# An induced-set attention with a gated convolution on one Trainium2 core: groups of 508 tokens with their own halo, h summed on VectorE, f16 output products in the last batch

## The chip, the core and the metric

The kernel runs on one core of a Trainium2 chip. TensorE (PE) multiplies matrices into PSUM, VectorE (DVE), ScalarE (ACT) and GpSimd (POOL) work elementwise, and SyncE's queue (SP) and ACT's queue issue the DMAs. The metric is the time on the device in microseconds (us), the median of several runs. A profiled execution gives the trace that the text reads.

## What is computed

```python
# x: (4, 12800, 128), inducing I: (32, 128); everything float32, weights come as float64
def mab(q, kv):
    s = scale * (q @ kv.T);  s = s - s.max(-1)
    a = exp(s);  a /= a.sum(-1) + 1e-09
    return a @ kv
h = mab(I, x)                  # per batch: 32 rows from 12800 tokens
y = mab(x, h)                  # 12800 tokens, softmax over 32
gate = sigmoid(causal 5-tap depthwise convolution of y by conv_w)
out  = (gate * (y @ w_val)) @ w_out
```

## The kernel before

The host passes x twice, in two layouts: `xT`, channels by tokens, and `xk`, tokens by channels. Each batch is cut into seven units: six big ones of 4 x 512 tokens and a small one of 4 x 128 (first in batch 0, last in the others; in stage 1 of batch 0 it is read last). Four groups of a unit lie side by side on PE's array, 32 rows each.

*Stage 1* of a batch makes h. For each unit: `load_t`, `load_k` (SP's queue); `a_mm` (scores of the 32 inducing rows, L236), `a_max` (L240), `a_exp` with its sum (L246), `a_tr` (128x128 transposes of the exponentials on PE, L252), `a_ev` (their copy out of PSUM by ACT, L257), `a_h` (the product with the tokens of `xk`, L265), `a_hev` (L271). Then the *preparation*: `p_nl` to `p_f` find the maximum over units and a factor f for each; `p_F` (L308) puts f on seven diagonal matrices and `p_h` (L319, L321) adds the seven units' h on PE with them; `p_hq`, `p_v`, `p_w` (L326 to L367), `p_wt`, `p_we` derive the scaled weights of the batch as f16 pairs (a high and a low half), and the output weights `wo` in f32.

*Stage 2* takes each unit through a chain: `b_mm` (scores against h, L389), `b_tr` (transposed by 32x32 blocks on DVE, L394), `b_max` (L399), `b_sub` (POOL, L404), `b_exp` (ACT, L409), `b_sum` (DVE, L414 to L416), `b_norm` (POOL, L421), `b_back` (DVE, L426), `b_hi` (ACT, f16 high half, L432), `b_lo` (POOL: f16 low half, L437, and the halo of four tokens in front of each group, copied from the end of the group before, L442 and L444). Then `c_gate` (60 f16 products of 32 rows: five taps, three passes each of high and low halves, four groups; L453) fills four PSUM banks, one a group; `c_tanh` reads them in two halves of two banks (L464); `c_val` (12 such products, the same L453 by its helper `strips`) fills the same four banks once both tanh are done; `c_gv` multiplies, in two halves (L473); `c_out` is the f32 product with `wo` for each group (L478), `c_ev` its copy by ACT (L485), and after the fourth comes the store (L487, ACT's queue).

The first half of batch b+1's stage 1 lies among the stage 2 units of batch b. The order on every engine is written out by a planner (`Plan.order`): each task has an engine, a duration, a key and its dependencies, and of the tasks that could start within `SLACK` of the earliest, the lowest key goes next. `BUFS` counts the buffers: 12 of `xT`, 4 of `xk`, 3 of `hl`, 2 PSUM banks `o` for outputs, one set of four banks `g` for gate and value.

Of the kernel before, what the change touches and what calls it, by code (L numbers as in the profile page):

```python
# [18 lines left out]
P = 128  # L19
M = 32  # L20
# [4 lines left out]
SP = 16384.0  # L25
TINY = 1e-30


def units(b):
    small = [(0, 128)] if b == 0 else [(12288, 128)]  # L30
    big = [(2048 * u + 512 * (b == 0), 512) for u in range(6)]
    return small + big if b == 0 else big + small

# [4 lines left out]
BUFS = dict(xT=12, xk=4, E=2, ET=2, q=3, m=2, z=2, p=2, hl=3, gt=4, os=2, hs=1, nm=3, wst=2, wst2=2, gsc=2, hq=2, s=1, x=1, o=2, g=1)  # L38
LAT = 0.15
SLACK = 0.1  # L40
OUTK = 1.4
KA, KB, KP, KS = -2.5, 0.6, 4.0, 1.3
# [9 lines left out]

class Plan:
# [79 lines left out]
def tile_kernel(ctx: ExitStack, tc: tile.TileContext, xT, xk, inducing, w_val, conv_w, w_out, out):  # L133
# [21 lines left out]
    def constants():  # L155
        warm = const.tile([P, 1], F32, name="warm")
        V.memset(warm, 0.0)
        S.activation(warm, warm, AF.Exp)
        ind = const.tile([M, P], F32, name="ind")
        nc.scalar.dma_start(ind, inducing)  # L160
        identf = const.tile([P, P], F32, name="identf")
        make_identity(nc, identf)
        ident = const.tile([P, P], F16, name="ident")
        V.tensor_copy(ident, identf)
        ones = const.tile([P, P], F32, name="ones")
        V.memset(ones, 1.0)
        id4 = const.tile([P, M], F32, name="id4")
# [50 lines left out]
    def load_t(b, u):  # L218
        t0, w = units(b)[u]
        x = st[b, u, "xT"] = sbt("xT", [P, G * 512])  # L220
        nc.sync.dma_start(x[:, :G * w], xT[b, :, t0:t0 + G * w])

    def load_k(b, u):
        t0, w = units(b)[u]
        n = G * w // P
        x = st[b, u, "xk"] = sbt("xk", [P, 16, P])
        nc.sync.dma_start(x[:, :n, :], xk[b, :, t0 // P:t0 // P + n, :])

    def a_mm(b, u):
        w = units(b)[u][1]  # L230
        if "nz" not in bat[b]:
            bat[b]["nz"] = sbt("nm", [P, 2, NU])
        sc = st[b, u, "s1"] = ps("s1", TAG1(b, u), [P, 512])
        x = st[b, u, "xT"]
        for g in range(G):
            T.matmul(sc[M * g:M * g + M, :w], c_["iw"], x[:, w * g:w * g + w], start=True, stop=True, tile_position=(0, M * g))  # L236
# [11 lines left out]
    def a_tr(b, u):  # L248
        w = units(b)[u][1]
        et = st[b, u, "etp"] = ps("et", "x", [P, 4, P])  # L250
        for i in range(w // P):
            T.transpose(et[:, i, :], st[b, u, "E"][:, P * i:P * i + P], c_["identf"])  # L252

    def a_ev(b, u):
        n = units(b)[u][1] // P
        et = st[b, u, "et"] = sbt("ET", [P, 4, P])
        S.copy(et[:, :n, :], st[b, u, "etp"][:, :n, :])  # L257

    def a_h(b, u):
        n = units(b)[u][1] // P  # L260
        hp = st[b, u, "h"] = ps("h", "x", [P, 512])
        et, x = st[b, u, "et"], st[b, u, "xk"]
        for i in range(n):
            for g in range(G):
                T.matmul(hp[M * g:M * g + M, :P], et[:, i, M * g:M * g + M], x[:, n * g + i, :],  # L265
                         start=i == 0, stop=i == n - 1, tile_position=(0, M * g))
# [49 lines left out]
    def p_h(b):
        d = bat[b]
        t = d["t"] = ps("t", TAGP(b), [P, 512])
        T.matmul(t[:, 256:256 + M], c_["ones"], d["zf"], start=True, stop=True)  # L319
        for u in range(NU):  # L320
            T.matmul(t[:, :M], d["hs"][:, u, :], d["F"][:, u, :], start=u == 0, stop=u == NU - 1)  # L321

# [15 lines left out]
    def p_w(b):  # L338
# [10 lines left out]
        V.tensor_scalar(vmx, vmx, TINY, 1.0 / SW, ALU.max, ALU.mult)  # L349
# [16 lines left out]
        wo = d["wo"] = sbt("wo", [P, P], tag="wst")  # L366
        V.tensor_scalar(wo, c_["w2"], vmx, 0.5 / SP, ALU.mult, ALU.mult)  # L367

# [15 lines left out]
    def b_mm(b, u):  # L384
        w = units(b)[u][1]
        sc = st[b, u, "s2"] = ps("s2", "s", [P, 512])
        x = st[b, u, "xT"]
        for g in range(G):
            T.matmul(sc[M * g:M * g + M, :w], bat[b]["hq"], x[:, w * g:w * g + w], start=True, stop=True, tile_position=(0, M * g))  # L389

    def b_tr(b, u):
        w = units(b)[u][1]
# [3 lines left out]
    def b_max(b, u):  # L396
        n = units(b)[u][1] // M
# [3 lines left out]
    def b_sub(b, u):  # L401
        n = units(b)[u][1] // M
# [3 lines left out]
    def b_exp(b, u):  # L406
        n = units(b)[u][1] // M
        q = st[b, u, "q"]
        S.activation(q[:, :n], q[:, :n], AF.Exp)  # L409

    def b_sum(b, u):
        n = units(b)[u][1] // M
        z = st[b, u, "z"] = sbt("z", [P, 16, 1])
        V.tensor_reduce(z[:, :n, 0], st[b, u, "q"][:, :n, :], AX.X, ALU.add)  # L414
        V.tensor_scalar(z[:, :n], z[:, :n], 1e-9, 1.0 / SP, ALU.add, ALU.mult)
        V.reciprocal(z[:, :n], z[:, :n])  # L416

    def b_norm(b, u):
        n = units(b)[u][1] // M
# [3 lines left out]
    def b_back(b, u):  # L423
        w = units(b)[u][1]
# [4 lines left out]
    def b_hi(b, u):  # L429
        w = units(b)[u][1]  # L430
        h = st[b, u, "hl"] = sbt("hl", [P, 2, 520], F16)
        S.copy(h[:, 0, 4:4 + w], st[b, u, "p"][:, :w])  # L432

    def b_lo(b, u):
        w = units(b)[u][1]
        h = st[b, u, "hl"]
        Gp.tensor_tensor(h[:, 1, 4:4 + w], st[b, u, "p"][:, :w], h[:, 0, 4:4 + w], ALU.subtract)  # L437
        if u == 0:
            Gp.memset(h[:M, :, 0:4], 0.0)
        else:  # L440
            v = units(b)[u - 1][1]
            Gp.tensor_copy(h[:M, :, 0:4], st[b, u - 1, "hl"][P - M:, :, v:4 + v])  # L442
        for g in range(1, G):
            Gp.tensor_copy(h[M * g:M * g + M, :, 0:4], h[M * g - M:M * g, :, w:4 + w])  # L444


    def strips(b, u, bank, d, k, first, last):
        w = units(b)[u][1]
        h, wst = st[b, u, "hl"], bat[b]["wst"]
        for i, (part, wp) in enumerate(((0, 0), (0, 1), (1, 0))):  # L450
            for g in range(G):
                s = slice(M * g, M * g + M)
                T.matmul(bank[:, g, :w], wst[s, wp, k, :], h[s, part, 4 - d:4 - d + w],  # L453
# [12 lines left out]
    def c_val(b, u):  # L466
        bank = st[b, u, "v"] = ps("v", "g", [P, G, 512])
        strips(b, u, bank, 0, TAPS, True, True)

    def c_gv(b, u, i):  # L470
        w = units(b)[u][1]
        t = st[b, u, i, "t"]
        V.scalar_tensor_tensor(t[:, :, :w], t[:, :, :w], 1.0, st[b, u, "v"][:, 2 * i:2 * i + 2, :w], ALU.add, ALU.mult)  # L473

    def c_out(b, u, g):
        w = units(b)[u][1]
        op = st[b, u, g, "o"] = ps("o", "o", [P, 512])
        T.matmul(op[:, :w], bat[b]["wo"], st[b, u, g // 2, "t"][:, g % 2, :w], start=True, stop=True)  # L478

    def c_ev(b, u, g):  # L480
# [4 lines left out]
        S.copy(os[:, w * g:w * g + w], st[b, u, g, "o"][:, :w])  # L485
# [16 lines left out]
    hl = {}  # L502
    hq = [None] * B
    ph = []
    wready = [None] * B

    def l(w, a, full):
        return a + (full - a) * w / 512

    def stage1(b):  # L510
# [23 lines left out]
        a = add("DVE", 1.05, k, p_F, (b,), deps=[a] + aexp)  # L534
        a = x = add("PE", 2.3, k, p_h, (b,), deps=[a] + hev, alloc=TAGP(b))
# [4 lines left out]
        a = add("DVE", 4.0, k, p_w, (b,), deps=[a, k2], uses=[x])  # L540
        for i in range(2):
# [5 lines left out]
    def stage2(b):  # L547
        nonlocal outs
        for u in range(NU):
# [11 lines left out]
            prev = [hl[b, u - 1]] if u else []  # L561
            lo = add("POOL", l(w, 1.05, 2.05), key, b_lo, (b, u), uses=[bk, hi] + [x[0] for x in prev], deps=[x[1] for x in prev])
            hl[b, u] = (hi, lo)
# [3 lines left out]
            va = add("PE", l(w, 0.19, 0.76), key - 0.3, c_val, (b, u), deps=th, uses=[hi], alloc="g")  # L567
# [59 lines left out]
```

## Time and profile before

| | |
|---|---|
| median of 3 runs | 352.07 us (351.9 to 355.13) |
| the profiled execution | 354.44 us, its span 352.7 us |
| busy: PE, DVE, ACT, POOL | 315.0, 197.9, 176.0, 103.3 us |
| HBM read, written | 52.71 MB, 26.21 MB |
| granted TensorE clock, mean | 0.974 |

The page gives the busy time of each engine and the span in 40 slices of 8.8 us, each digit a tenth. Groups of instructions are named by line, engine and operation, with their count, busy time and mean duration; f32 products appear as two records each.

### The profile page before, as it was taken

What the parts mean: (1) busy time and instruction counts of PE and PEld (TensorE: products, weight loads), DVE (VectorE), ACT (ScalarE), POOL (GpSimd) and SP (SyncE); (2) the same over time, 40 slices, a digit from 0 to 9 for tenths busy, and PEclk for the clock granted to TensorE, in tenths of its full rate; (3) what the DMA queues carried; (4) which work ended last, traced back from release to release, by engine and by line L of the source; (5) the groups of instructions that cost most, each with busy time, mean ns of one, the idle gap of its engine ahead of it and who ended that gap; (6) DMA issues with size and microseconds to landing.
All of it is one profiled execution on the core that took longest, in us unless ns stands there. A gap on an engine that the chain in (4) does not pass through costs nothing.

```text
span 352.7 us, 8776 instructions
## 1 busy us (share of the span) xinstructions
PE 315.0 (89%) x3722; PEld 139.3 (39%) x3722; DVE 197.9 (56%) x415; ACT 176.0 (50%) x314; POOL 103.3 (29%) x202
## 2 busy tenths in 40 slices
PE   2475698989999999999999999999999999887774
PEld 0333455543343454343353444443354333332332
DVE  1432356656579773664678563666667758722220
ACT  1223313556553647466553557465654555624443
POOL 0000003434531443144431123443451457721000
PEclk9989959999999999999999999999999999989999
DMA  7999999838983293698983394012223230232233
GB/s 306 419 419 413 419 415 421 315 159 326 388 360 121 70 391 120 227 336 302 414 354 123 106 390 164 32 62 103 93 106 122 121 124 26 119 121 121 119 121 150
DMA packets 12481, 79.49 MB, mean 225 GB/s; under 512 B 1397, under 2 KB 1690, under 8 KB 3226
## 3 DMA queue, kind: packets, MB, share of 16 engines
q1 hardware_dynamic: 8064, 52.43, 38.2%
q10 hardware_dynamic: 4378, 26.50, 18.4%
q8 instruction: 29, 0.48, 0.6%
q14 instruction: 10, 0.08, 0.1%
HBM read 52.71 MB, written 26.21 MB: 224 GB/s over the span
## 4 chain that ended last, share of the span: by engine, by line
PE 79%; ACT 7%; DMA 7%; DVE 5%; issue 1%; ACTq 0%; SPq 0%; DVEq 0%
PE o L478 25%; PE g L453 24%; PE s L389 7%; PE s L236 6%; PE h L265 6%; PE v L453 4%; DMA xT<-in_xt_dram 4%; PE et L252 3%; ACT gt L464 3%; DMA raw<-in_moe_w_out_dram 3%; DVE gt L473 2%; PE t L321 2%; ACT os L485 2%; ACT E L246 1%; DVE nm L240 1%
## 5 line engine op out<-in xcount | busy, mean ns | idle before, releaser
L478 PE MATMUL o<-gt,wo 128*128 128x512 f32 (+1 forms) x224 | 105.0, 584 | 9.1 <-DVE gt L473 8.5
L453 PE MATMUL g<-hl,wstk 32*128 32x512 f16 (+1 forms) x1680 | 86.3, 352 | 0.0
L485 ACT COPY os<-o 128x512 f32<-128x512 f32 (+1 forms) x112 | 58.9, 542 | 50.6 <-PE o L478 49.9
L473 DVE SCALAR_TENSOR_TENSOR gt<-gt,v 128x1024 f32<-128x1024 f32 (+1 forms) x56 | 59.5, 1103 | 41.8 <-ACT os L485 30.1
L453 PEld LDWEIGHTS <-wstk 32*128 32x128 f16 x2016 | 44.7, 92 | 75.2 <-issue 19.3
L464 ACT ACTIVATE gt<-g,gsc 128x1024 f32<-128x1024 f32 (+1 forms) x56 | 54.4, 1019 | 35.0 <-PE g L453 26.8
L478 PEld LDWEIGHTS o<-gt,wo 128*128 128x128 f32 x224 | 36.1, 190 | 53.0 <-issue 32.7
L404 POOL TENSOR_TENSOR q<-q,m 128x512 f32<-128x512 f32 (+1 forms) x28 | 26.7, 955 | 103.2 <-DVE m L399 102.3
L421 POOL TENSOR_TENSOR q<-q,z 128x512 f32<-128x512 f32 (+1 forms) x28 | 26.7, 954 | 70.0 <-DVE z L416 50.6
L437 POOL TENSOR_TENSOR hl<-p,hl 128x512 f16<-128x512 f32 (+1 forms) x28 | 29.6, 1057 | 39.0 <-ACT hl L432 38.8
L246 ACT ACTIVATE E<-s,nm 128x512 f32<-128x512 f32 (+1 forms) x28 | 18.0, 643 | 34.8 <-DVE nm L240 27.1
L265 PE MATMUL h<-xk,ET 128*32 128x128 f32 x800 | 29.7, 289 | 2.5 <-ACT ET L257 2.5
L236 PE MATMUL s<-xT,iw 128*32 128x512 f32 (+1 forms) x224 | 30.7, 624 | 0.6 <-DMA xT<-in_xt_dram 0.3
L240 DVE TENSOR_REDUCE nm<-s 128x1 f32<-128x512 f32 (+1 forms) x28 | 17.6, 630 | 24.3 <-PE s L236 24.1
L265 PEld LDWEIGHTS h<-xk,ET 128*32 128x32 f32 x800 | 23.0, 117 | 17.6 <-ACT ET L257 10.6
L252 PE MATMUL et<-identf,E 128*128 128x128 f32 x100 | 18.1, 303 | 12.8 <-ACT E L246 12.0
L432 ACT CAST hl<-p 128x512 f16<-128x512 f32 (+1 forms) x28 | 16.1, 575 | 26.4 <-DVE p L426 25.1
L389 PE MATMUL s<-xT,hq 128*32 128x512 f32 (+1 forms) x224 | 27.6, 562 | 1.0 <-DVE q L394 1.0
L394 DVE STREAM_TRANSPOSE q<-s 128x512 f32<-128x512 f32 (+1 forms) x28 | 18.1, 645 | 13.3 <-PE s L389 13.2
L426 DVE STREAM_TRANSPOSE p<-q 128x512 f32<-128x512 f32 (+1 forms) x28 | 17.9, 646 | 11.9 <-POOL q L421 10.7
L453 PE MATMUL v<-hl,wstk 32*128 32x512 f16 (+1 forms) x336 | 21.2, 354 | 1.9 <-ACT gt L464 1.9
L409 ACT ACTIVATE q<-q 128x512 f32<-128x512 f32 (+1 forms) x28 | 16.4, 589 | 13.0 <-POOL q L404 12.5
(85 smaller groups left out, 194.8 us busy)
## 6 DMA issues: line engine op xcount, KB each, us to landing
xT<-in_xt_dram SPq DMA_DIRECT2D x24, 1024.0 KB, 9.5
xk<-in_xk_dram SPq DMA_DIRECT2D x24, 1024.0 KB, 11.4
out_dram<-os ACTq DMA_DIRECT2D x24, 1024.0 KB, 4.5
xT<-in_xt_dram SPq DMA_DIRECT2D x4, 256.0 KB, 8.7
xk<-in_xk_dram SPq DMA_DIRECT2D x4, 256.0 KB, 6.3
out_dram<-os ACTq DMA_DIRECT2D x4, 256.0 KB, 2.0
raw<-in_moe_w_val_dram ACTq DMA_DIRECT2D x1, 128.0 KB, 7.6
raw<-in_moe_w_out_dram ACTq DMA_DIRECT2D x1, 128.0 KB, 10.1
```

Of the source, the lines that this page charges most:

```text
L236: T.matmul(sc[M * g:M * g + M, :w], c_["iw"], x[:, w * g:w * g + w], start=True, stop=True, tile_position=(0, M * g))
L252: T.transpose(et[:, i, :], st[b, u, "E"][:, P * i:P * i + P], c_["identf"])
L265: T.matmul(hp[M * g:M * g + M, :P], et[:, i, M * g:M * g + M], x[:, n * g + i, :], start=i == 0, stop=i == n - 1, tile_position=(0, M * g))
L389: T.matmul(sc[M * g:M * g + M, :w], bat[b]["hq"], x[:, w * g:w * g + w], start=True, stop=True, tile_position=(0, M * g))
L404: Gp.tensor_tensor(q[:, :n], q[:, :n], st[b, u, "m"][:, :n].broadcast_to([P, n, M]), ALU.subtract)
L421: Gp.tensor_tensor(q[:, :n], q[:, :n], st[b, u, "z"][:, :n].broadcast_to([P, n, M]), ALU.mult)
L437: Gp.tensor_tensor(h[:, 1, 4:4 + w], st[b, u, "p"][:, :w], h[:, 0, 4:4 + w], ALU.subtract)
L453: T.matmul(bank[:, g, :w], wst[s, wp, k, :], h[s, part, 4 - d:4 - d + w], start=first and i == 0, stop=last and i == 2, tile_position=(M * ...
L464: S.activation(t[:, :, :w], st[b, u, "g"][:, 2 * i:2 * i + 2, :w], AF.Tanh, scale=bat[b]["gsc"])
L473: V.scalar_tensor_tensor(t[:, :, :w], t[:, :, :w], 1.0, st[b, u, "v"][:, 2 * i:2 * i + 2, :w], ALU.add, ALU.mult)
L478: T.matmul(op[:, :w], bat[b]["wo"], st[b, u, g // 2, "t"][:, g % 2, :w], start=True, stop=True)
L485: S.copy(os[:, w * g:w * g + w], st[b, u, g, "o"][:, :w])
```

## The change

- Units become 6 x 4 x 508 and 1 x 4 x 152 tokens. Each group computes its second scores for its own halo as well (four tokens more in big groups, eight in the small one: 512 and 160 wide), so the halo copies of `b_lo` go. `xT` gets eight zero columns in front, and each load takes eight columns more.
- `xk` is laid in blocks of 127 tokens (76 in the small unit), of which the load takes full 128 rows: 104 blocks a batch instead of 100.
- `p_F` and the seven products of `p_h` become `p_z`, seven `p_hs` on DVE (multiply by f and add) and one product with a stack of identities.
- The output weights leave `p_w` and are made by five steps `p_o1` to `p_o5`: scaled, transposed on PE, scaled by rows on DVE, transposed back, copied; a scale `osc` goes into `c_ev`. In the last batch they become an f16 pair `wh`.
- In the last batch `c_val` comes in two halves, one behind each tanh; `c_gh` (DVE) and `c_gl` (POOL) split the product into f16 halves, and `c_out` is three f16 products for each group. In the other batches the output product stays f32.
- One `xT` buffer fewer (11), new pools for the halves, and other keys for the planner: one addition for each kind of task, and other constants.

```diff
 def units(b):
-    small = [(0, 128)] if b == 0 else [(12288, 128)]
-    big = [(2048 * u + 512 * (b == 0), 512) for u in range(6)]
+    small = [(0, 152)] if b == 0 else [(12192, 152)]
+    big = [(2032 * u + 608 * (b == 0), 508) for u in range(6)]
...
+def halo(w):
+    return 4 if w == 508 else 8
+def block(w):
+    return 127 if w == 508 else 76
...
-BUFS = dict(xT=12, xk=4, ..., wst=2, wst2=2, gsc=2, hq=2, s=1, x=1, o=2, g=1)
+BUFS = dict(xT=11, xk=4, ..., wst2=2, gsc=2, osc=2, wh=2, wf32=2, gh=2, gl=2, hq=2, s=1, x=1, o=2, g=1)
+KEYS = dict(a_ev=-0.62, a_exp=-0.37, ...)
...
+def NVAL(b):
+    return 2 if b == 3 else 1
+def HALVES(b, i):
+    return b == 3
...
+    def p_hs(b, i):
+        d = bat[b]
+        u = (i + 1) % NU if b == 0 else i
+        if i == 0:
+            d["ha"] = sbt("ha", [P, P])
+            V.tensor_scalar(d["ha"], d["hs"][:, u, :], d["f"][:, u], None, ALU.mult)
+        else:
+            V.scalar_tensor_tensor(d["ha"], d["hs"][:, u, :], d["f"][:, u], d["ha"], ALU.mult, ALU.add)
     def p_h(b):
...
-        for u in range(NU):
-            T.matmul(t[:, :M], d["hs"][:, u, :], d["F"][:, u, :], start=u == 0, stop=u == NU - 1)
+        T.matmul(t[:, :M], d["ha"], c_["id4"], start=True, stop=True)
...
     def b_mm(b, u):
...
-            T.matmul(sc[M * g:M * g + M, :w], bat[b]["hq"], x[:, w * g:w * g + w], ...)
+            o = PAD + w * g
+            T.matmul(sc[M * g:M * g + M, :wide(w)], bat[b]["hq"], x[:, o - halo(w):o + w], ...)
...
     def b_sum(b, u):
...
-        V.tensor_scalar(z[:, :n], z[:, :n], 1e-9, 1.0 / SP, ALU.add, ALU.mult)
+        V.scalar_tensor_tensor(z[:, :n], z[:, :n], 1.0 / SP, c_["eps"][:, :n], ALU.mult, ALU.add)
...
     def b_lo(b, u):
...
-            Gp.tensor_copy(h[:M, :, 0:4], st[b, u - 1, "hl"][P - M:, :, v:4 + v])
-        for g in range(1, G):
-            Gp.tensor_copy(h[M * g:M * g + M, :, 0:4], h[M * g - M:M * g, :, w:4 + w])
...
+    def c_val(b, u, i):
+        n = NVAL(b)
+        strips(b, u, st[b, u, "g"], 0, TAPS, True, True, range(G // n * i, G // n * i + G // n))
...
+    def c_gh(b, u, i):
+        h = st[b, u, i, "gh"] = sbt("gh", [P, 2, 512], F16)
+        V.tensor_copy(h[:, :, :w], st[b, u, i, "t"][:, :, :w])
+    def c_gl(b, u, i):
+        l = st[b, u, i, "gl"] = sbt("gl", [P, 2, 512], F16)
+        Gp.tensor_tensor(l[:, :, :w], st[b, u, i, "t"][:, :, :w], st[b, u, i, "gh"][:, :, :w], ALU.subtract)
     def c_out(b, u, g):
...
+        wh = bat[b]["wh"]
+        for i, (x, k) in enumerate((("gh", 0), ("gh", 1), ("gl", 0))):
+            T.matmul(op[:, :w], wh[:, k, :], st[b, u, g // 2, x][:, g % 2, :w], start=i == 0, stop=i == 2)
     def c_ev(b, u, g):
...
-        S.copy(os[:, w * g:w * g + w], st[b, u, g, "o"][:, :w])
+        S.activation(os[:, w * g:w * g + w], st[b, u, g, "o"][:, :w], AF.Copy, scale=bat[b]["osc"])
...
+                    gh = add("DVE", l(w, 0.1, 0.84), key - 0.4, c_gh, (b, u, i), deps=[gv], uses=[th[i]], alloc="gh")
+                    gl = add("POOL", l(w, 0.2, 2.2), key - 0.4, c_gl, (b, u, i), uses=[th[i], gh], alloc="gl")
```

More of the change, by code (lines that the diff above doesn't have):

```diff
@@ L24, with wide, blocks @@
 SW = 1024.0
-SP = 16384.0
+SV = 16.0
+SP = 1024.0
 TINY = 1e-30
+PAD = 8
 def units(b):
-    small = [(0, 128)] if b == 0 else [(12288, 128)]
-    big = [(2048 * u + 512 * (b == 0), 512) for u in range(6)]
+    small = [(0, 152)] if b == 0 else [(12192, 152)]
+    big = [(2032 * u + 608 * (b == 0), 508) for u in range(6)]
     return small + big if b == 0 else big + small
+def halo(w):
+    return 4 if w == 508 else 8
+def wide(w):
+    return w + halo(w)
+def block(w):
+    return 127 if w == 508 else 76
+def blocks(b, u):
+    return sum(G * w // block(w) for _, w in units(b)[:u])
 NU = 7
-BUFS = dict(xT=12, xk=4, E=2, ET=2, q=3, m=2, z=2, p=2, hl=3, gt=4, os=2, hs=1, nm=3, wst=2, wst2=2, gsc=2, hq=2, s=1, x=1, o=2, g=1)
+BUFS = dict(xT=11, xk=4, E=2, ET=2, q=3, m=2, z=2, p=2, hl=3, gt=4, os=2, hs=1, nm=3, wst2=2, gsc=2, osc=2, wh=2, wf32=2, gh=2, gl=2, hq=2, s=1, x=1, o=2, g=1)
 LAT = 0.15
-SLACK = 0.1
-OUTK = 1.4
-KA, KB, KP, KS = -2.5, 0.6, 4.0, 1.3
+KEYS = dict(a_ev=-0.62, a_exp=-0.37, a_hev=-0.82, a_max=0.97, a_mm=0.08, b_back=-0.14, b_exp=0.34, b_hi=0.7,
+            b_lo=-0.38, b_max=-0.28, b_sub=0.28, b_sum=0.95, b_tr=-0.54, c_ev=0.84, c_gl=0.36, c_out=0.2,
+            c_tanh=-0.25, const_iw=-0.8, conv_max=-1.25, load_k=0.97, load_t=0.74, p_F=-2.83, p_f=1.38,
+            p_h=-0.04, p_hq=1.05, p_hs=-0.03, p_nM=-0.59, p_nMc=-0.7, p_nt=-1.37, p_o1=-0.86, p_o2=-1.13,
+            p_o3=0.76, p_o4=1.1, p_o5=-0.21, p_row=0.54, p_v=-0.14, p_w=4.39, p_we=-0.86, p_wt=0.4)
+SLACK = 0.07
+OUTK = 2.35
+KA, KB, KP, KS = -3.26, 0.74, 4.57, 1.7
 def TAG1(b, u):
@@ L249, in a_tr @@
         w = units(b)[u][1]
+        k = block(w)
         et = st[b, u, "etp"] = ps("et", "x", [P, 4, P])
-        for i in range(w // P):
-            T.transpose(et[:, i, :], st[b, u, "E"][:, P * i:P * i + P], c_["identf"])
+        for i in range(w // k):
+            T.transpose(et[:k, i, :], st[b, u, "E"][:, k * i:k * i + k], c_["identf"])
     def a_ev(b, u):
-        n = units(b)[u][1] // P
+        w = units(b)[u][1]
+        k, n = block(w), w // block(w)
         et = st[b, u, "et"] = sbt("ET", [P, 4, P])
-        S.copy(et[:, :n, :], st[b, u, "etp"][:, :n, :])
+        S.copy(et[:k, :n, :], st[b, u, "etp"][:k, :n, :])
     def a_h(b, u):
-        n = units(b)[u][1] // P
+        w = units(b)[u][1]
+        k, n = block(w), w // block(w)
         hp = st[b, u, "h"] = ps("h", "x", [P, 512])
@@ L365, in p_w, with p_o1, p_o2, p_o3 @@
         V.tensor_scalar(gsc, gmx, 0.5 / SP, None, ALU.mult)
-        wo = d["wo"] = sbt("wo", [P, P], tag="wst")
-        V.tensor_scalar(wo, c_["w2"], vmx, 0.5 / SP, ALU.mult, ALU.mult)
+        d["vmx"] = vmx
+    def p_o1(b):
+        d = bat[b]
+        wo = d["wo"] = sbt("wo", [P, P])
+        V.tensor_scalar(wo, c_["w2"], d["vmx"], None, ALU.mult)
+    def p_o2(b):
+        d = bat[b]
+        t = d["ot"] = ps("t", TAGP(b), [P, 512])
+        T.transpose(t[:, :P], d["wo"], c_["identf"])
+    def p_o3(b):
+        d = bat[b]
+        cs = d["cs"] = sbt("cs", [P, 1])
+        V.tensor_reduce(cs, d["ot"][:, :P], AX.X, ALU.max, apply_absolute_value=True)
+        V.tensor_scalar(cs, cs, TINY, 1.0 / SW, ALU.max, ALU.mult)
+        rs = sbt("rs", [P, 1])
+        V.reciprocal(rs, cs)
+        V.tensor_scalar(d["wo"], d["ot"][:, :P], rs, None, ALU.mult)
+        osc = d["osc"] = sbt("osc", [P, 1])
+        V.tensor_scalar(osc, cs, 0.5 / SP, None, ALU.mult)
+    def p_o4(b):
+        d = bat[b]
+        T.transpose(d["ot"][:, P:2 * P], d["wo"], c_["identf"])
+    def p_o5(b):
+        d = bat[b]
+        if any(HALVES(b, i) for i in range(2)):
+            wh = d["wh"] = sbt("wh", [P, 2, P], F16)
+            V.tensor_copy(wh[:, 0], d["ot"][:, P:2 * P])
+            V.tensor_tensor(wh[:, 1], d["ot"][:, P:2 * P], wh[:, 0], ALU.subtract)
+        if not all(HALVES(b, i) for i in range(2)):
+            wf32 = d["wf32"] = sbt("wf32", [P, P])
+            V.tensor_copy(wf32, d["ot"][:, P:2 * P])
     def p_wt(b, i):
@@ L401, in b_sub @@
     def b_sub(b, u):
-        n = units(b)[u][1] // M
+        n = wide(units(b)[u][1]) // M
         q = st[b, u, "q"]
@@ L406, in b_exp @@
     def b_exp(b, u):
-        n = units(b)[u][1] // M
+        n = wide(units(b)[u][1]) // M
         q = st[b, u, "q"]
@@ L429, in b_hi, with strips @@
     def b_hi(b, u):
-        w = units(b)[u][1]
-        h = st[b, u, "hl"] = sbt("hl", [P, 2, 520], F16)
-        S.copy(h[:, 0, 4:4 + w], st[b, u, "p"][:, :w])
+        w = wide(units(b)[u][1])
+        h = st[b, u, "hl"] = sbt("hl", [P, 2, 512], F16)
+        S.copy(h[:, 0, :w], st[b, u, "p"][:, :w])
     def b_lo(b, u):
-        w = units(b)[u][1]
+        w = wide(units(b)[u][1])
         h = st[b, u, "hl"]
-        Gp.tensor_tensor(h[:, 1, 4:4 + w], st[b, u, "p"][:, :w], h[:, 0, 4:4 + w], ALU.subtract)
+        Gp.tensor_tensor(h[:, 1, :w], st[b, u, "p"][:, :w], h[:, 0, :w], ALU.subtract)
         if u == 0:
-            Gp.memset(h[:M, :, 0:4], 0.0)
-        else:
-            v = units(b)[u - 1][1]
-            Gp.tensor_copy(h[:M, :, 0:4], st[b, u - 1, "hl"][P - M:, :, v:4 + v])
-        for g in range(1, G):
-            Gp.tensor_copy(h[M * g:M * g + M, :, 0:4], h[M * g - M:M * g, :, w:4 + w])
-    def strips(b, u, bank, d, k, first, last):
+            Gp.memset(h[:M, :, 0:halo(units(b)[u][1])], 0.0)
+    def strips(b, u, bank, d, k, first, last, groups=range(G)):
         w = units(b)[u][1]
@@ L450, in strips @@
         for i, (part, wp) in enumerate(((0, 0), (0, 1), (1, 0))):
-            for g in range(G):
+            for g in groups:
                 s = slice(M * g, M * g + M)
-                T.matmul(bank[:, g, :w], wst[s, wp, k, :], h[s, part, 4 - d:4 - d + w],
+                T.matmul(bank[:, g, :w], wst[s, wp, k, :], h[s, part, halo(w) - d:halo(w) - d + w],
                          start=first and i == 0, stop=last and i == 2, tile_position=(M * g, 0))
@@ L501, in tile_kernel @@
     last = k0
-    hl = {}
     hq = [None] * B
@@ L533, in stage1 @@
         a = add("ACT", 0.3, k, p_f, (b,), deps=[a])
-        a = add("DVE", 1.05, k, p_F, (b,), deps=[a] + aexp)
-        a = x = add("PE", 2.3, k, p_h, (b,), deps=[a] + hev, alloc=TAGP(b))
+        z = add("DVE", 0.6, k, p_z, (b,), deps=[a] + aexp)
+        for i in range(NU):
+            a = add("DVE", 0.23, k, p_hs, (b, i), deps=[a, hev[i]])
+        a = x = add("PE", 0.6, k, p_h, (b,), deps=[a, z], alloc=TAGP(b))
         ph.append(a)
@@ L560, in stage2 @@
             hi = add("ACT", l(w, 0.2, 0.6), key, b_hi, (b, u), uses=[bk], alloc="hl")
-            prev = [hl[b, u - 1]] if u else []
-            lo = add("POOL", l(w, 1.05, 2.05), key, b_lo, (b, u), uses=[bk, hi] + [x[0] for x in prev], deps=[x[1] for x in prev])
-            hl[b, u] = (hi, lo)
+            lo = add("POOL", l(w, 0.3, 1.18), key, b_lo, (b, u), uses=[bk, hi])
             key += KS
@@ L566, in stage2 @@
             th = [add("ACT", l(w, 0.26, 1.11), key - 0.5, c_tanh, (b, u, i), uses=[ga], alloc="gt") for i in range(2)]
-            va = add("PE", l(w, 0.19, 0.76), key - 0.3, c_val, (b, u), deps=th, uses=[hi], alloc="g")
+            if NVAL(b) == 1:
+                va = [add("PE", l(w, 0.19, 0.76), key - 0.3, c_val, (b, u, 0), deps=th, uses=[hi, ga])] * 2
+            else:
+                va = [add("PE", l(w, 0.17, 0.7), key - 0.3, c_val, (b, u, i), deps=[th[i]], uses=[hi, ga]) for i in range(2)]
             for o, g in outs:
```

77 lines of the change are left out of this document (45 added, 32 removed).

## The prediction

> **What bounds the kernel now.** I read the page's shares and slices first, then the busy time of each engine in three stretches, then the order of time inside the last one.
>
> ```profile
> PE 315.0 (89%) x3722; PEld 139.3 (39%) x3722; DVE 197.9 (56%) x415; ACT 176.0 (50%) x314; POOL 103.3 (29%) x202
> PE   2475698989999999999999999999999999887774
> DMA  7999999838983293698983394012223230232233
> ```
>
> ```profile
> 0.00:64.00 64.00, 42.26 (x588) 23.87 (x588) 26.64 (x82) 17.91 (x42) 4.29 (x15) 0.89 0.99 402
> 64.00:281.00 217.00, 215.36 (x2546) 92.76 (x2536) 141.02 (x288) 123.57 (x215) 78.41 (x147) 1.00 0.55 211
> 281.00:352.70 71.70, 57.39 (x601) 22.62 (x600) 30.20 (x47) 34.56 (x58) 20.64 (x41) 0.97 0.28 111
> ```
>
> The columns of the second fence are the stretch, PE, PE's weight loads, DVE, ACT, POOL, the granted clock, the DMA share and GB/s. There are three regimes. Up to 64 us the DMA is the bound (0.99 busy) and PE idles 21.7 us. From 64 to 281 us PE idles 1.6 us of 217: only less PE work helps there. From 281 us, where the last batch's seven units are all that is left, PE idles 14.3 us and nothing else is full: this stretch is held by a loop of waits. One turn of that loop in order of time:
>
> ```profile
> 281.20 3.42 PE L453 MATMUL g<-hl,wstk 32*128 32x512 f16 x60
> ...
> 310.21 3.52 PE L478 MATMUL o<-gt,wo 128*128 128x512 f32 x4 [1.49 <-DVE gt L473]
> ...
> 313.66 3.50 PE L453 MATMUL g<-hl,wstk 32*128 32x512 f16 x60
> ...
> 323.59 3.42 PE L453 MATMUL g<-hl,wstk 32*128 32x512 f16 x60
> 326.94 1.98 PE L478 MATMUL o<-gt,wo 128*128 128x512 f32 x4
> 327.06 2.12 ACT L464 ACTIVATE gt<-g,gsc 128x1024 f32<-128x1024 f32 x2 [2.78 <-PE g L453]
> 329.23 0.83 PE L453 MATMUL v<-hl,wstk 32*128 32x512 f16 x12 [0.31 <-ACT gt L464]
> 330.17 2.35 DVE L473 SCALAR_TENSOR_TENSOR gt<-gt,v 128x1024 f32<-128x1024 f32 x2 [7.49 <-ACT os L485]
> 331.54 1.96 PE L478 MATMUL o<-gt,wo 128*128 128x512 f32 x4 [1.48 <-DVE gt L473]
> 333.43 3.42 PE L453 MATMUL g<-hl,wstk 32*128 32x512 f16 x60
> 343.27 1.02 PE L453 MATMUL g<-hl,wstk 32*128 32x128 f16 x60
> 349.39 0.34 ACTq L487 DMA_DIRECT2D out_dram<-os  x1
> ```
>
> Gate (3.4 us), both tanh (2.1), value after the second tanh (0.8), product of the first half (1.2), two output matmuls (2.0), next gate: 9.84 us a turn (323.59 to 333.43). Six turns, from 281.20 to 343.27, take 62.1 us, of which 1.6 us is a stretch of slower clock (3.52 us at 310.21 for what is 1.96 us elsewhere). The small unit and the last store take the remaining 9.4 us.
>
> **The change, part by part.** The rows that price it:
>
> ```profile
> L478 PE MATMUL o<-gt,wo 128*128 128x512 f32 x192 | 99.0, 630 | 7.9 <-DVE gt L473 7.4 <-ACT E L246 0.5
> L453 PE MATMUL g<-hl,wstk 32*128 32x512 f16 x1440 | 82.2, 375 | 0.0
> L252 PE MATMUL et<-identf,E 128*128 128x128 f32 x100 | 18.1, 303 | 12.8 <-ACT E L246 12.0 <-DVE gt L473 0.5 <-DVE hs L271 0.3
> L321 PE MATMUL t<-F,hs 128*128 128x32 f32 x56 | 7.5, 289 | 0.0
> L473 DVE SCALAR_TENSOR_TENSOR gt<-gt,v 128x1024 f32<-128x1024 f32 x48 | 56.5, 1217 | 36.4 <-ACT os L485 25.6 <-PE v L453 8.9 <-ACT hl L432 1.5
> L473 DVE SCALAR_TENSOR_TENSOR gt<-gt,v 128x256 f32<-128x256 f32 x8 | 3.0, 417 | 5.3 <-ACT os L485 4.6 <-ACT hl L432 0.7
> L362 DVE CAST wr<-wf 128x768 f16<-128x768 f32 x4 | 2.2, 560 | 0.1
> L164 DVE CAST ident<-identf 128x128 f16<-128x128 f32 x1 | 0.2, 227 | 0.5 <-POOL identf masks.py:199 0.5
> L437 POOL TENSOR_TENSOR hl<-p,hl 128x512 f16<-128x512 f32 x24 | 27.9, 1162 | 28.9 <-ACT hl L432 28.9
> L404 POOL TENSOR_TENSOR q<-q,m 128x512 f32<-128x512 f32 x24 | 25.1, 1048 | 45.8 <-DVE m L399 44.9 <-PE o L478 0.2
> L437 POOL TENSOR_TENSOR hl<-p,hl 128x128 f16<-128x128 f32 x4 | 1.7, 429 | 10.1 <-ACT hl L432 9.8
> L444 POOL COPY hl<-hl 32x8 f16<-32x8 f16 x84 | 15.4, 183 | 4.9
> L485 ACT COPY os<-o 128x512 f32<-128x512 f32 x96 | 55.1, 588 | 45.0 <-PE o L478 44.3
> L409 ACT ACTIVATE q<-q 128x512 f32<-128x512 f32 x24 | 15.2, 636 | 8.7 <-POOL q L404 8.2 <-ACT os L485 0.4
> ```
>
> *Groups with their own halo.* The 84 halo copies (and the 24 of line 442, taken as alike) leave POOL: 108 x 0.18 = 19.8 us, and with them the wait of one unit on the one before. POOL is 29% busy and PE waits for it nowhere after 64 us, so this is worth nothing by itself; it makes room on POOL, which the last batch then needs. The columns on PE stay 12,800 a batch for gate, value and output; the second scores have 128 more (1%). The small unit gets two transposes for one (0.18 us) and eight h products for four (0.25 us): with the wider scores about +0.5 us of PE a batch.
>
> *h summed on DVE.* The 14 records a batch of line 321 (7.5 / 4 = 1.9 us of PE) become 2 (0.27): -1.6 us a batch. Seven DVE operations of 128 elements come in; by the two forms of line 473 ((1217 - 417) / 768 = 1.04 ns an element) one is 0.28 us, 2.0 us in series. Two 128x128 transposes of the scaled output weights come to PE (18.1 / 100 = 0.18 us each, up to 0.3 alone), so 0.4 to 0.6 us. Net for PE -1.1 us a batch, and in batches 1 to 3 the score products that need h come later than h, so the 2 us on DVE are covered; uncovered they would show whole. With the small unit: 3 x (-1.1 + 0.5) = **-1.8 us** in the full stretch. The planner's new keys change every engine's order there too; an order moves no work off PE, it can only open gaps: 0 to +2 us, I take 0. ACT's eviction gains a scale: between 588 and 636 ns, at most 1.3 us a batch on an engine half idle: nothing, and 0.2 us a turn should ACT ever carry the loop.
>
> *Loads.* The DMA is the bound up to 64 us. Per batch, four blocks of 64 KB and 56 columns of 512 B are added, 0.29 MB; at 402 GB/s that is 0.7 us a batch. One xT buffer fewer makes the load that goes out at 40.81 us wait as the next one does, until 50.33:
>
> ```profile
> 40.81 0.43 SPq L221 DMA_DIRECT2D xT<-in_xt_dram  x1
> 50.33 0.33 SPq L221 DMA_DIRECT2D xT<-in_xt_dram  x1
> xT<-in_xt_dram SPq DMA_DIRECT2D x24, 1024.0 KB, 9.5
> ```
>
> Everything behind it on SP's queue, the xk loads too, waits with it. A load lands 9.5 us after its issue, so the engines would run dry for 0 to 2 us. Rows of 8160 in place of 8192 bytes, off their old boundaries, have no row here; from nothing to the 2% that the bytes already grew. Against this, batch 0 saves 1.6 us of PE between 43 and 46 us (with 2 us of DVE in exchange) and 0.7 us of halo copies ahead of its first gate. **Head: -1 to +3 us, I take +0.8.**
>
> *The last batch.* Three f16 passes take the place of an f32 product: 0.95 us (1.96 / 2 above; 99.0 / 96 = 1.03 over the run) becomes 3 x 0.224 = 0.67 us (the gate's 15 passes in 3.36 us). PE per unit: 3.4 + 0.8 + 2.7 = 6.9 us for 8.1. Value by two banks lets the first half's value and product run beside the second tanh. The turn becomes: gate 3.36, first tanh 1.06, half value 0.42, product 1.2, second product 1.2, with some 0.5 us of hand-overs: **7.8 us**, the output products of the unit before lying in the gaps (2.7 us in 3.6). New on DVE: two casts of 1024, by the two CAST rows (0.52 ns an element) 0.69 us each. New on POOL: two differences of 1024, by line 437 (1.91 ns an element) 2.14 us each, 4.3 us a unit.
>
> What stands against it is what POOL and DVE do to each other:
>
> ```profile
> 292.03 0.17 DVE L415 TENSOR_SCALAR z<-z 128x16 f32<-128x16 f32 x1
> 292.63 1.05 POOL L421 TENSOR_TENSOR q<-q,z 128x512 f32<-128x512 f32 x1 [3.68 <-DVE z L416]
> 293.07 0.64 DVE L415 TENSOR_SCALAR z<-z 128x16 f32<-128x16 f32 x1
> ```
>
> The same small operation takes 0.17 us alone and 0.64 us when POOL is at work: it ends at 293.71, just after POOL's ends at 293.68. The product (line 473), which reads PSUM, shows no such thing. The new cast is a one-source operation from SBUF to SBUF at twice the element rate of line 473, like line 415's kind, so I count casts and POOL's work as one queue. While a unit of the first scores' chain is still to be done for each unit put out, that queue holds 2 x 1.05 + 1.16 + 2 x 2.14 + 2 x 0.69 + 0.17 = 9.1 us a turn; once the chains are done (before: POOL's last instruction is near 322 us), 4.28 + 1.38 = 5.7 us. So three turns at 9.2 us and three at 7.9 (7.8 and a little for casts): 51.3 us for 62.1, **-10.8 us**. Alone, by the loop without that queue, it would be 6 x 7.8 = 46.8 us (-15.3).
> The Trainium skill, "SBUF — State Buffer", section "SBUF: two separate sides", says why: VectorE in a two-port mode, or with two SBUF inputs, and GpSimd take one port pair as an exclusive lock for a whole instruction. The trace agrees (0.17 and 0.64 us). By the same sentence the seven new h operations, with two SBUF inputs, would be held too; no row here shows that.
>
> *The end.* The small unit's outputs now pass cast, POOL difference and three passes, behind the big unit's two differences of 2.14 us: from the last gate, 5.3 us until those are done, 1.2 for the small ones, 0.6 for output and eviction, 3.3 to the end as now (349.39 to 352.7): 10.4 us for 9.4, **+1.0**.
>
> Sum: -10.8 + 1.0 - 1.8 + 0.8 = -10.8 us. The profiled execution took 354.44 us for its span of 352.7; the median shown is 352.07, 2.4 us lower. 343.6 in the profile's terms is 341.3 as a median; I say 341.5.
>
> **The rivals.** *The shared queue costs more than its sum.* In-order POOL puts a 2.14 us difference ahead of a score step, and the chain it delays delays the gate: the first three turns stay at 10.8 us and the later ones take 8.9: 59.1 us, -3.0, with the other terms -3.0: 349.1. For it: 9.1 us of work in a 9.2 us turn leaves no slack. Against: before, the chains were ahead by up to 20 us (POOL done by 322, last gate at 343).
> *Slower.* If DVE's order has a cast ahead of the second product, that product waits for the cast, and the cast for a POOL difference: 2.14 + 0.69 = 2.8 us on the loop, 10.6 us a turn, six turns 63.6 (+1.5), and +1.0, the head's upper 3 us, -1.8: +3.7, 355.8. It decides against the change once that wait is over 1.9 us a turn. Against it: the second half's value is there before the first product ends.
> *No cheaper passes.* If the weight loads of three passes with changing weights show (0.1 us each), a product costs as much as now, and PE's 8.1 us and its gaps set the turn at about 8.8: three turns of +0.9 = +2.7, the first three hidden: -8.1, 344.
> *Better.* The queue costs nothing because the chains run far enough ahead: -15.3 + 1.0 - 1.8 and 0 at the head: -16.1, 336.
>
> **How the numbers follow.** Forecast (339 to 346) 0.48, shared queue 0.20, slower 0.12, no cheaper passes 0.07, better 0.13. One per cent is 3.5 us (the three runs shown lie 3.2 us apart, so less can't be told from no change). Faster: 0.48 + 0.13 + 0.07 and a quarter of 0.20 = 0.73; within: 0.15; slower: 0.12. The range goes from the better case's lower side, 334, to 352, which leaves out the slower case and some edges.
>
> **What would show it.** After: gates in the last batch 7.8 to 8 us apart at the end and about 9 before; f16 output triples of 0.67 us; casts of 0.69 us alone and up to 2.8 us beside POOL; POOL near 43 us after the last batch's first gate (20.6, less 24 copies = 4.4, and 27 of differences); PE still without gaps from the mid sixties on. PE gaps between 45 and 80 us, or gates of the last batch 10 us apart with casts ahead of products, would make the prediction wrong.

## The result, and the profile after

The changed kernel takes 363.0 us (median of 4 runs, 361.8 to 367.71) against 352.03 us before: slower, ratio 1.028 with a 95% interval of 1.020 to 1.036. The forecast was 341.5 us.

The page of the changed kernel: shares, slices of 9 us, and the granted clock.

```profile
span 359.8 us, 8798 instructions
PE 317.0 (88%) x3746; PEld 138.7 (39%) x3746; DVE 223.2 (62%) x479; ACT 186.6 (52%) x314; POOL 112.2 (31%) x108
PE   2567588999999999999999989999999988777784
PEclk9988969999999999999999999999999999997868
```

The same stretches as before, that from 64 to 281 us in two pieces (stretch, PE, weight loads, DVE, ACT, POOL, clock, DMA share, GB/s):

```profile
0.00:64.00 64.00, 41.88 (x547) 23.44 (x547) 32.66 (x98) 17.89 (x42) 5.37 (x13) 0.89 0.98 407
64.00:80.00 16.00, 15.21 (x267) 8.52 (x264) 10.56 (x22) 9.05 (x20) 6.55 (x6) 1.00 0.65 241
80.00:281.00 201.00, 198.60 (x2317) 83.04 (x2305) 139.62 (x305) 122.09 (x197) 58.92 (x61) 1.00 0.55 213
281.00:359.80 78.80, 61.29 (x631) 23.66 (x630) 40.36 (x57) 37.62 (x58) 41.38 (x29) 0.91 0.25 101
```

Up to 281 us little has changed: from 64 us on PE has 1.6 us less work (213.81 us for 215.36) and 1.6 us more of gaps. The loss is in the last stretch, 78.8 us instead of 71.7, at a clock of 0.91 instead of 0.97. In order of time, one turn of the last batch and the start of the next ones:

```profile
282.12 3.40 PE L533 MATMUL g<-hl,wstk 32*128 32x508 f16 x60
...
320.94 3.40 PE L533 MATMUL g<-hl,wstk 32*128 32x508 f16 x60
324.44 2.11 ACT L544 ACTIVATE gt<-g,gsc 128x1016 f32<-128x1016 f32 x2 [1.77 <-PE g L533]
326.60 0.82 PE L533 MATMUL g<-hl,wstk 32*128 32x508 f16 x6 [0.88 <-ACT gt L544]
327.53 1.21 DVE L554 SCALAR_TENSOR_TENSOR gt<-gt,g 128x1016 f32<-128x1016 f32 x1 [5.21 <-PE g L533]
328.79 1.45 PE L533 MATMUL g<-hl,wstk 32*128 32x508 f16 x6 [1.37 <-DVE gt L554]
330.18 1.03 PE L575 MATMUL o<-gh,wh 128*128 128x508 f16 x2
330.28 1.21 DVE L554 SCALAR_TENSOR_TENSOR gt<-gt,g 128x1016 f32<-128x1016 f32 x1 [1.54 <-PE g L533]
332.83 4.44 PE L533 MATMUL g<-hl,wstk 32*128 32x508 f16 x60
345.52 1.17 PE L533 MATMUL g<-hl,wstk 32*128 32x152 f16 x60
```

The reader is to see two things. The first half of the value (326.60) starts only when **both** tanh are done (326.55), and the second half (328.79) waits for the **first product** (327.53 to 328.74), which reads the other two banks. So the two halves run one after the other, each with its product behind it. And from 328.79 us on PE itself is slow in stretches: 1.45 us for what is 0.82 us two rows above, 4.44 us for a gate of 3.40.

Against the kernel before, the first gate of the last batch comes 0.9 us later (282.12 for 281.20), six turns take 63.4 us for 62.1, and from the last gate to the end pass 14.3 us for 9.4: 0.9 + 1.3 + 4.9 = 7.1 us, the difference of the spans. The medians lie 11.0 us apart and not 7.1, mostly because the profiled execution before was 2.4 us above its median and the one after 1.2 us below.

### The profile page after: what moved, and what is told of

The parts are those of the page before. It is cut to its first block, busy times and chain, and to the rows that moved or that the text cites. A ratio compares the mean times of both kernels' runs of the same rounds, so it can differ in the third digit from the quotient of the medians.

```text
span 359.8 us, 8798 instructions
## 1 busy us (share of the span) xinstructions
PE 317.0 (88%) x3746; PEld 138.7 (39%) x3746; DVE 223.2 (62%) x479; ACT 186.6 (52%) x314; POOL 112.2 (31%) x108
## 4 chain that ended last, share of the span: by engine, by line
PE 72%; DVE 11%; DMA 6%; ACT 6%; issue 3%; ACTq 0%; POOL 0%; DVEq 0%; POOLq 0%
PE g L533 29%; PE o L571 17%; PE h L308 7%; PE s L474 5%; PE s L276 5%; PE et L293 4%; PE o L575 4%; DMA out_dram<-os 3%; DMA raw<-in_moe_w_out_dram 3%; ACT gt L544 3%; DVE gt L554 2%; DVE nm L280 1%; ACT os L582 1%; ACT E L286 1%; DVE m L484 1%
## 5 line engine op out<-in xcount | busy, mean ns | idle before, releaser
L533 PE MATMUL g<-hl,wstk 32*128 32x508 f16 (+1 forms) x2016 | 114.6, 357 | 13.5 <-DVE gt L554 7.1
L582 ACT ACTIVATE os<-o,osc 128x508 f32<-128x508 f32 (+1 forms) x112 | 69.7, 641 | 44.2 <-PE o L575 21.3
L554 DVE SCALAR_TENSOR_TENSOR gt<-gt,g 128x1016 f32<-128x1016 f32 (+1 forms) x56 | 60.2, 1103 | 36.9 <-PE g L533 35.2
L571 PE MATMUL o<-gt,wf 128*128 128x508 f32 (+1 forms) x168 | 78.8, 575 | 0.1
L544 ACT ACTIVATE gt<-g,gsc 128x1016 f32<-128x1016 f32 (+1 forms) x56 | 55.1, 1021 | 35.5 <-PE g L533 29.8
L565 POOL TENSOR_TENSOR gl<-gt,gh 128x1016 f16<-128x1016 f32 (+1 forms) x14 | 28.1, 2015 | 30.6 <-DVE gh L560 27.5
L571 PEld LDWEIGHTS o<-gt,wf 128*128 128x128 f32 x168 | 26.7, 190 | 25.8 <-issue 14.9
L308 PE MATMUL h<-xk,ET 127*32 127x128 f32 (+1 forms) x832 | 31.5, 295 | 3.8 <-ACT ET L299 3.6
L308 PEld LDWEIGHTS h<-xk,ET 127*32 127x32 f32 (+1 forms) x832 | 23.9, 118 | 19.9 <-ACT ET L299 11.3
L276 PE MATMUL s<-xT,iw 128*32 128x508 f32 (+1 forms) x224 | 30.7, 624 | 0.8 <-DVE q L479 0.5
```

Source lines behind the costliest of these rows:

```text
L276: T.matmul(sc[M * g:M * g + M, :w], c_["iw"], x[:, PAD + w * g:PAD + w * g + w], start=True, stop=True, tile_position=(0, M * g))
L308: T.matmul(hp[M * g:M * g + M, :P], et[:k, i, M * g:M * g + M], x[:k, n * g + i, :], start=i == 0, stop=i == n - 1, tile_position=(0, M * g))
L533: T.matmul(bank[:, g, :w], wst[s, wp, k, :], h[s, part, halo(w) - d:halo(w) - d + w], start=first and i == 0, stop=last and i == 2, tile_p ...
L544: S.activation(t[:, :, :w], st[b, u, "g"][:, 2 * i:2 * i + 2, :w], AF.Tanh, scale=bat[b]["gsc"])
L565: Gp.tensor_tensor(l[:, :, :w], st[b, u, i, "t"][:, :, :w], st[b, u, i, "gh"][:, :, :w], ALU.subtract)
L571: T.matmul(op[:, :w], bat[b]["wf32"], st[b, u, g // 2, "t"][:, g % 2, :w], start=True, stop=True)
```

## The experiments

The first theory was that the waits are made for a whole tile: the four banks of gate and value are one tile (one piece of memory to the program, which sets the waits), so a write to two of its banks waits for every earlier read of the other two. The rivals were the queue of DVE and POOL, and the f16 passes.

**Two tiles of two banks.** The order on every engine stays as it is in the changed kernel.

```diff
...
-                T.matmul(bank[:, g, :w], wst[s, wp, k, :], ...)
+                T.matmul(bank[g // 2][:, g % 2, :w], wst[s, wp, k, :], ...)
...
-        bank = st[b, u, "g"] = ps("g", "g", [P, G, 512])
+        bank = st[b, u, "g"] = [ps("g0", "g0", [P, 2, 512]), ps("g1", "g1", [P, 2, 512])]
...
```

> The changed kernel with gate and value in two PSUM tiles of two banks instead of one tile of four; planner, order and arithmetic unchanged. Theory (the half value's waits are made for the whole tile: first half for both tanh, second half for the first product): the turn in the last batch falls from 9.9 to 12.7 us to 7.8 to 8.3 us, the PE clock stays near 1.0 since PE is then over 90% busy, time 344 to 350 us. Rival 1 (DVE's casts and POOL's differences hold the loop by their shared queue): turns stay at 9.5 us or more, 357 us or more. Rival 2 (the slow clock comes from the three f16 passes themselves): turns begin near 8 us but the clock still drops to 0.75, 350 to 356 us.

345.87 us (344.42 to 347.79), 0.976 of the kernel before (0.970 to 0.981). The turn in order of time:

```profile
314.09 3.52 PE L533 MATMUL g<-hl,wstk 32*128 32x508 f16 x60
317.58 2.11 ACT L544 ACTIVATE gt<-g,gsc 128x1016 f32<-128x1016 f32 x2 [1.35 <-PE g L533]
318.93 1.62 PE L533 MATMUL g<-hl,wstk 32*128 32x508 f16 x12
319.86 2.34 DVE L554 SCALAR_TENSOR_TENSOR gt<-gt,g 128x1016 f32<-128x1016 f32 x2 [3.99 <-PE g L533]
321.88 3.76 PE L533 MATMUL g<-hl,wstk 32*128 32x508 f16 x60
329.84 0.24 PE L533 MATMUL g<-hl,wstk 32*128 32x152 f16 x2
```

The value now starts while the second tanh runs (318.93, tanh until 319.69), both products follow without a gap, and the turn is 7.79 us; six turns take 48.8 us (281.04 to 329.84), the clock stays at 1.0 (stretches of 10 us from 280 to 340). Both rivals fall, although POOL is busy without a gap from 300 to 320 us:

```profile
300.00:310.00 10.00, 9.99 (x115) 4.18 (x108) 9.66 (x17) 7.25 (x12) 10.00 (x8) 1.00 0.47 197
310.00:320.00 10.00, 9.87 (x99) 4.79 (x99) 4.33 (x7) 7.01 (x10) 10.00 (x7) 1.00 0.26 106
```

**The same once more**, beside the run with the products moved (below).

> The kernel with two tiles once more, on the same chip as the run beside it, so that the two can be compared: 344 to 348 us by the theory, turns 7.8 to 8.3 us; if the gain of the first run was the chip's, 350 us or more.

346.52 us, 0.980 (0.972 to 0.988): the gain is there again.

**The value whole in the last batch** (`NVAL` returns 1), f16 halves kept.

> The changed kernel with the value in one piece in the last batch, as in the other batches; f16 output halves stay; the planner orders anew. Theory: value waits for both tanh as in the kernel before, but costs 0.8 us once instead of 0.8 us twice, and no half waits for the first product: turn 3.4 + 2.3 + 0.8 + 2.4 + 0.2 = 9.0 us, 352 to 357 us if the clock holds. Rival (the slow clock follows from a PE that is busy under 80%): PE has 6.8 us of work in a 9 us turn, the clock falls to 0.75 to 0.85 over most of the last batch and the time stays at 357 to 363 us.

350.9 us, 0.989 (0.985 to 0.994); turns of 8.94 to 9.00 us in the second half of the batch. A little better than the theory said. The clock held at 1.0 although PE was busy only 70 to 80% there, so the rival's rule, a slow clock whenever PE is busy under 80%, is wrong as it stands.

**Neither last-batch part** (`NVAL` returns 1, `HALVES` returns False).

> The changed kernel without both last-batch parts (value in one piece, f32 outputs everywhere); own halos, h on DVE, full-row loads, planner keys and 11 buffers stay. Theory: the rest of the change costs what the first gate of the last batch shows (282.1 us for 281.2, +0.9 us), turns 9.8 us: 351 to 355 us. Rival: the rest of the change carries a loss of its own in the end stretch (keys, scaled evictions): 357 us or more.

354.47 us, 0.997 (0.993 to 1.001): own halos, h on DVE, the new loads and the new keys together change nothing that can be measured (at most 0.7%).

**Two tiles, f32 outputs** (`HALVES` returns False).

> The changed kernel with two PSUM tiles, half values in the last batch, but f32 outputs everywhere (no casts, no POOL differences). Theory: PE has 3.4 + 1.6 + 3.8 = 8.8 us a turn and becomes the bound: turns 8.9 to 9.1 us, clock near 1.0, 345 to 349 us; the f16 halves are then worth some 5 us (against two tiles with f16). Rival (the half value at full price eats what the overlap gives): turns at 9.8 us, 351 to 355 us.

348.31 us, 0.983 (0.977 to 0.990): turns of 8.5 us at the end (316.86, 325.41, 333.94), PE over 99% busy from 290 to 330 us. Against the run with neither part that is 6 us, but the planner's order differs too, so overlap alone isn't shown to give them: the run with one tile and f32 outputs (next) has this run's order and no overlap, and stands at 0.989 for 0.983, with intervals that overlap. With f16 halves the median is 2.4 us lower still, half of what I had expected, and there too the intervals overlap.

**One tile, f32 outputs** (`HALVES` returns False, all else as in the changed kernel).

> The changed kernel with one tile of four banks and half values, but f32 outputs everywhere. Theory (the half values in one tile are the loss, whatever the output): first half behind both tanh, second behind the first product, two f32 products of 1.9 us behind that: turns 10.3 to 10.7 us, against 9.8 with the value whole: 357 to 361 us, with the clock nearer 1.0 than with f16 outputs, since PE does more. Rival (the f16 halves are the loss): turns 9.8 us, 352 to 356 us.

349.13 us, 0.989 (0.984 to 0.993). Both sides of the expectation fall: the halves in one tile are no loss here. The trace shows the difference:

```profile
318.21 3.40 PE L533 MATMUL g<-hl,wstk 32*128 32x508 f16 x60
...
323.82 0.84 PE L533 MATMUL g<-hl,wstk 32*128 32x508 f16 x12 [0.31 <-ACT gt L544]
...
324.79 2.34 DVE L554 SCALAR_TENSOR_TENSOR gt<-gt,g 128x1016 f32<-128x1016 f32 x2 [6.64 <-PE g L533]
...
327.19 3.40 PE L533 MATMUL g<-hl,wstk 32*128 32x508 f16 x60
```

Both halves stand behind both tanh, as one tile would have it, but they run back to back in 0.84 us, and neither waits for a product; the turn is 8.98 us. Without casts, the planner had put the first product behind both halves in program order. So the theory had to be narrowed: a write waits for those reads of the tile that stand ahead of it in program order, that is, were written out earlier.

**The first product behind both halves**, in the changed kernel (one tile, f16).

```diff
-                gv = add("DVE", ..., c_gv, (b, u, i), uses=[th[i], va[i], ga])
+                gv = add("DVE", ..., c_gv, (b, u, i), uses=[th[i], va[1], ga])
```

> The changed kernel (one tile of four banks, half values, f16 outputs), with one dependency more in the planner: the first product of a unit stands behind both half values in program order, as it came to stand by itself in the run with one tile and f32 outputs (349.1 us, both halves back to back behind both tanh, no wait on the first product). Theory (a write to the second half of the tile waits for every earlier read of the tile in program order, so it is the place of the first product between the halves that costs): no wait of value for a product, turns 8.9 to 9.1 us, clock near 1.0, 350 to 353 us, like the run with the value whole. Rival (half values in one tile with f16 outputs are slow whatever the order): turns 9.8 us or more, 357 us or more.

352.37 us, 0.997 (0.992 to 1.001), turns of 8.97 to 9.03 us from 304.90 to 340.91, clock 1.0. The narrowed theory holds: one dependency more brings the changed kernel from 1.028 to 0.997 of the kernel before. It doesn't give the overlap, which only two tiles do.

**PE's gaps filled** in the changed kernel, for what the slow clock costs. From the third unit of the last batch on, eight matmuls a unit write a bank that nobody reads.

```diff
...
+        if filled:
+            c_["fill"] = ps("fill", "s", [P, 512])
+            fill(b, u, 3)
         strips(b, u, st[b, u, "g"], 0, TAPS, True, True, range(G // n * i, G // n * i + G // n))
+        if filled:
+            fill(b, u, 5)
```

> The changed kernel (one tile of four banks) with eight f16 matmuls a unit added in the last batch from the third unit on, whose result nobody reads: three in PE's wait ahead of the first half value, five in its wait ahead of the second; 1.8 us of PE in 2.2 us of gaps. Theory (the waits hold the loop, and the slow clock follows from a PE array that does too little): turns stay at 9.9 to 10.1 us, the granted clock stays at 0.98 to 1.0 up to the last gate, and the time falls by what the slow clock cost, to 356 to 359 us. Rival (the slow clock comes from the f16 passes or by chance, whatever fills the gaps): clock again 0.75 to 0.9 in the last 40 us, 361 to 368 us.

355.89 us, 1.012 (1.004 to 1.020). Of the two lines, the first is from the run with PE's gaps filled and the second from the changed kernel, in the same stretch:

```profile
330.00:340.00 10.00, 9.57 (x94) 3.80 (x93) 3.62 (x5) 4.58 (x6) 4.50 (x2) 1.00 0.26 106
```

```profile
330.00:340.00 10.00, 9.12 (x80) 3.23 (x79) 4.13 (x3) 3.98 (x6) 4.22 (x2) 0.75 0.25 104
```

Turns stay at 9.9 to 10.0 us (300.99 to 340.85), no longer and no shorter, and the clock holds at 1.0 (over the whole span 0.978 to 0.985 in the four runs; in the changed kernel's four, 0.961 to 0.966 in three and 0.948 in the one of 367.71 us): more work on PE makes the kernel faster. That divides the loss of one tile against two: by the medians 363.0 - 355.9 = 7 us of slow clock and 355.9 - 346.5 = 9 us of waits, by the ratios (1.028, 1.012, 0.980) some 6 and 11 us; the kernel before ran 2 to 3 us slower beside these runs than beside the changed kernel. The traces give 6.1 us for the clock: turns of 11.89 and 12.69 us for 9.94, and 14.3 us from the last gate to the end for 12.85.

**f32 at the end**: two tiles, f16 halves for five big units, f32 for the last two (`return b == 3 and u < 5`).

> Two PSUM tiles and f16 halves as in the run with two tiles, but f32 outputs for the last big unit and the small one. Theory (the end pays for casts and POOL differences that nothing hides: 12.9 us from the last gate to the end for 9.4 in the kernel before): the end falls to 9.5 to 10.5 us, one turn grows by 0.5 to 1 us, 342.5 to 345 us. Rival (the end is set by PE and evictions behind it, not by casts): the end stays at 12 us or more, 345 to 347 us.

344.92 us, 0.981 (0.973 to 0.989): not to be told from the run with two tiles. From the last gate to the end pass 12.4 us (330.89 to 343.3), hardly less than 12.9 with casts. The rival holds: casts are not what sets the end. In the changed kernel's order all four outputs of the last big unit stand behind the small unit's gate, with their evictions, where the kernel before has two of them ahead of it. The traces go by that count: two outputs behind the gate, 9.4 us to the end (before, and with neither part); three, 11.1 to 11.2 us (both runs with f32 outputs and half values); four, 12.4 us here and 12.5 to 12.9 us with casts at the full clock. No run moved the outputs alone.

## Why the prediction was wrong

**The step that failed** is the sentence that value by two banks lets the first half's value and product run beside the second tanh. With it fails the reason given against the slower case, that the second half's value is there before the first product ends: it started at 328.79 us, behind the product's end at 328.74. I took the dependencies that the data have for those that the program has. In one tile the first half still waits for both tanh, and as the first product stands between the halves in program order, the second half waits for it too. In place of 7.8 to 9.2 us the turn was 9.9 us after a first one of 9.0, and 11.9 and 12.7 us at the slow clock. With the waits gone, the turns I had worked out are there: 7.7 to 9.0 us, 48.8 us in six turns, between my 51.3 and the loop's 46.8. The kernel then gains 7 to 9 us where some 10.6 were forecast, and the end alone, below, takes 2.5 us more than I had put in.

**Half a value.** I counted 0.42 us for two groups of four. It is 0.82 us, as for all four (0.83): four strips of 32 rows run side by side on the array, and two take as long. This term, mis-sized by 0.4 us twice a turn, costs PE 0.8 us a unit. In one tile it lies on the loop; in two tiles PE is busy without a gap (10.00 of 10 us from 320 to 330 us), and whether a cheaper half would shorten the turn no run shows.

**The slow clock** was missing from the sum; I had seen one such stretch in the kernel before (1.6 us) and put nothing in for it. It cost 6 to 7 us.

**The end** was said to grow by 1.0 us and grew by 4.9 in the changed kernel, by 3.5 us with two tiles (12.9 for 9.4). Casts and differences, which I counted, aren't the main part: without them 12.4 us are left. The order of the outputs, which I didn't look at, fits the other runs, as said above, and was not tried by itself.

**The rivals.** The slower case (0.12) gave 355.8 us and named a wait of the second product for a cast ahead of it. The sign was right and the mechanism was not: the second product waits for its value, and the casts come behind both products. (Its break-even is off as well: by its own figures a wait of 2.2 us a turn, 2.8 - 3.7 / 6, not 1.9, would have brought the gain to nothing.) The shared queue is real. Cast, POOL's difference and cast, in the changed kernel:

```profile
331.41 0.68 DVE L560 CAST gh<-gt 128x1016 f16<-128x1016 f32 x1
...
332.24 2.11 POOL L565 TENSOR_TENSOR gl<-gt,gh 128x1016 f16<-128x1016 f32 x1 [5.69 <-DVE gh L560]
...
332.57 2.32 DVE L560 CAST gh<-gt 128x1016 f16<-128x1016 f32 x1 [0.48 <-PE o L575]
```

The second cast takes 2.32 us for 0.68, and ends 0.54 us after POOL's instruction (334.35): held by it, as foreseen. But the next gate waits for products only, so it cost the turns nothing; with two tiles, three turns of 8.98, 8.02 and 7.73 us stood where I had put 9.2 each.

**What was right.** Three f16 passes take 0.66 us (0.67 said), the cast 0.68 (0.69), the difference 2.11 (2.14). The rest of the change (-1.8 and +0.8 us said) can't be told from nothing. The loads in rows of 8160 bytes are as fast as the old ones (407 GB/s up to 64 us for 402), so that head cost stays small. The eviction with a scale was outside its bounds, 0.68 us for 0.59 to 0.64:

```profile
L582 ACT ACTIVATE os<-o,osc 128x508 f32<-128x508 f32 x96 | 64.2, 684 | 39.0 <-PE o L575 20.7 <-PE o L571 13.3 <-DMA out_dram<-os 4.1
L364 DVE SCALAR_TENSOR_TENSOR ha<-hs,f,ha 128x128 f32<-128x128 f32 x24 | 9.2, 385 | 0.8
```

The second line is the h sum on DVE, 0.385 us each for 0.28 said; in batch 0 PE waits 2.62 us behind it (until 44.81 us), which the head's sum had allowed for as 2 us. The mean holds one sum of 1.19 us, for some 0.36 elsewhere: it began with a POOL instruction (248.25 us, 1.05 us long) and ended 0.14 us after it. That is the row that was missing for h sums being held.

## What to carry to other kernels

Where a part of a buffer is to be reused early, make that part a tile of its own, or put every write to it ahead of the first read of its neighbour in program order, which spares the extra wait but gives no overlap (352.4 us here, for 346.5 with two tiles). A plan that knows the data's dependencies says nothing on those that the program will have. Read the first instruction of the new overlap in the trace and what it waited for, before anything else. And a loop that leaves an engine's array idle can pay twice, once for the wait and once in the clock.

## What the runs showed of the hardware

PE's granted clock fell to 0.75 in stretches of 10 us though no gap of PE in the turns was longer than 1.4 us. The Trainium skill, "TensorE: Matmul & The Clock Gate", section "HAM oscillation — how this bites in real kernels", gives gaps of more than some 3.4 us as the condition; these runs differ. The next section of that page of the Trainium skill, "A second HAM failure mode: psum-queue depth-cycling", has frequent short gaps switch the clock as well; the changed kernel's trace agrees (gaps of 0.8 to 1.4 us, clock 0.75). Filling 1.8 us of 2.2 us of gaps a turn kept the clock at 1.0, so the f16 passes alone don't bring it down, and the gaps have a part in it. Where the bound lies stays open: with the value whole PE was busy 70 to 80%, with gaps of 2.0 us in a turn of 9.0, and the profiled clock held. The work of the array per turn (gate, value and outputs over the turn, a half value counted half) was (3.4 + 0.8 + 2.6) / 9.9 = 0.69 where the clock fell and 6.8 / 9.0 = 0.76 where it held; that such a share is what counts was not tried, and it can't be all: in the kernel before, with a share of (3.4 + 0.8 + 3.9) / 9.8 = 0.83, the clock fell to 0.83 from 310 to 320 us.
